# Row numbers of routed tokens: one-hot blocks as weights in all phases instead of a row that is turned

## The chip, the core and the metric

The kernel runs on one core of a Trainium2 chip. The time is that of one launch on the device, in microseconds (us); three runs of the kernel before gave 591.25, 592.46 and 592.63 us, median 592.46. TensorE (PE) multiplies matrices and loads its weights beside that (PEld), VectorE is DVE, ScalarE is ACT, GpSimd is POOL, and SyncE (SP) issues most transfers. Each engine works through its own instructions in order.

## The reference, cut to what matters

Attention with a window and four sink positions gives 1536 tokens of 512 values. They are routed to eight experts, and a second network runs over the result.

```python
cap = N // E                                  # 1536 // 8 = 192
for idx in np.argsort(-(x @ w_gate).flatten()):
    tok, e = idx // E, idx % E
    if assigned[tok] >= 0 or counts[e] >= cap: continue
    assigned[tok] = e; counts[e] += 1
for e in range(E):
    mask = assigned == e
    out[mask] = np.maximum(x[mask] @ w1[e], 0.0) @ w2[e]
# then: h = out @ w_in; g = max(h, 0) + alpha * min(h, 0); result = g @ w_out
```

Every expert receives exactly 192 tokens, so which tokens an expert receives depends on all experts that were full before it.

## The kernel before, in words

**Stages.** Attention comes first. Then eight routing phases (`phase`, s = 0 to 7) each close one expert: compare logits over all tokens still alive, count, pick the expert that is full first, and give its 192 tokens a rank. Phases 0 and 1 look at 12 blocks of 128 tokens, phases 2 and 3 at 9, phases 4 to 7 at 6, because after every second phase (0 and 1, 2 and 3) the living tokens are packed together (`compact`: logits go to memory by indirect transfers on POOL and come back on SP). Expert products (`expert`, L1658 in float32 for experts 0 to 3, L1665 in halves of float16 for experts 4 to 7) and the second network (`chunk`, L1800 and L1843, one chunk for two experts, 384 tokens) run while later phases still route.

**From rank to tokens.** For each block c of a phase DVE makes a one-hot block `o.tile[:, c, a]` of 128 tokens by 192 places in float16 (`hot`, L1325). Both phases of a pair (a = 0, 1) write their half of one buffer `ohs`, of which there is a single one. `gather` (L1470) turns this into token numbers in `sidx`, one number on each partition and three columns for the 384 tokens of a pair: column 0 is filled by the even phase, column 1 by both, 64 numbers each, column 2 by the odd phase. POOL then fetches the tokens' rows from memory with two indirect transfers (L1530), PE turns them (L1543), and the expert's products can begin.

**The two ways to the numbers.** For s >= `BY_ROW` (L1481 to L1500) each block gives one product: weights `tok[:, c:c+1]` (128x1, float16, the token numbers), moving the one-hot block (192 columns), summed over the blocks into one row of 192 on a single partition (L1485). ACT copies the row out of PSUM (L1492), two transposes of 1x128 or 1x64 bring it upright (L1497), and DVE casts it to integers (L1516, L1519, L1521). For s < `BY_ROW` (L1501 to L1514) each block gives two products (only one in phase 0): weights a 128x128 or 128x64 piece of the one-hot pair, moving the token numbers, one column (L1507); the sums stand upright in PSUM and go to the casts at once. In the odd phase the piece for column 1 holds 64 places of either phase, so these products also read the even phase's one-hots. A task covers up to four blocks.

**What sets the order.** All instructions are issued in an order that a planner (`Plan.run`) writes out before the launch. A task has a set of engines, an estimated duration, and a rank: the longest way from it to the end, with `boost` added along the way and `urge` on top of its own rank alone. On each engine the planner takes the task that can start first by its own estimates, and between tasks that can start at the same time the one of the higher rank. `lag` holds a task back by so much behind its inputs. The product tasks of experts and chunks form a chain, so that the earlier ones have the higher rank. Index tasks of the row way have `urge=self.urge(s)` and `lag=self.lag(s)`, which are 300 and 1.0 us for s >= 2, and planned durations of 0.1 us for each block and 0.2 us for the turn. Those of the column way have `urge=self.chain(s)` and a lag of 45 us in phase 0 alone; `chain` is 900 for s = 1 and 0 otherwise; the planned duration is 0.052 us for each block.

**PSUM.** The index sums stand in a bank of the ring `r_r`, which has two. The bank is held from the first product to the last cast. The same ring serves the broadcasts (L1154) and counts (L1221) of the routing and the turned rows (L1543) of phases 1 to 7.

Of the kernel before, what the change touches and what calls it, by code (L numbers as in the profile page):

```python
# [91 lines left out]
class Plan:  # L92
# [11 lines left out]
    def task(self, eng, fn, r=(), w=(), behind=None, after=(), tail=0.0, boost=0.0, nbytes=0, pre=None, bias=None, urge=0.0, port=False, lag=0.0):  # L104

        t = Task()
        t.port = {"DVE": port, "POOL": not tail}
        t.urge, t.lag = urge, lag  # L110
        t.eng, t.fn, t.tail, t.boost, t.n = eng, fn, tail, boost, len(self.tasks)
        deps = set(after)
        t.nbytes, t.pre, t.bias = nbytes, pre, self.BIAS if bias is None else bias
        for x in r:
            deps.update(x.writers)
        for x in w:
            deps.update(x.writers)
            deps.update(x.readers)
        for x in r:
            x.readers.append(t)  # L120
        for x in w:
            x.writers, x.readers = [t], []
        t.bufs = []
        for x in (*r, *w):
            if x.buf is not None:
                if t not in x.buf.users:
                    x.buf.users.append(t)
                if x.buf not in t.bufs:
                    t.bufs.append(x.buf)
        deps.discard(t)  # L130
        t.behind = behind if behind not in deps else None
        if behind is not None:
            deps.add(behind)
        t.deps = list(deps)
        t.succ, t.start, t.end, t.by = [], None, None, None
        for d in t.deps:
            d.succ.append(t)
        self.tasks.append(t)
        return t
# [851 lines left out]
class Routed:  # L991
# [13 lines left out]
    LAND = 4.0  # L1005
    WAIT = 24
    HOT = (40.0,) + (0.0,) * 7
    BY_ROW = 2
    HOLD = {8: 0}
    BY_PE = (0,)  # L1010
    PICK, SET = 300.0, 2000.0
# [260 lines left out]
    def build(self, ctx, w1, w2, weights, out, x16, isv, sv_res):  # L1272
# [197 lines left out]
        def gather(s, st, o, parts):  # L1470
# [9 lines left out]
            rows = ((0, 0, 128), (1, 0, 64)) if not a else ((1, 64, 128), (2, 0, 128))  # L1480
            for x, ro in enumerate(parts) if s >= self.BY_ROW else ():  # L1481

# [6 lines left out]
                named = task({"PE": 0.1 * min(4, nb - 4 * x)}, index, r=[ro, st.t_res], w=got[-1:], urge=self.urge(s), lag=self.lag(s))  # L1489
            if s >= self.BY_ROW:  # L1490
                row, half = idrow[g], idrow[g].part(a)
# [8 lines left out]
                task({"PE": 0.2}, upright, r=[half, idrow[g].part(0)], w=got, urge=self.urge(s), lag=self.lag(s))  # L1500
            for x, ro in enumerate(parts) if s < self.BY_ROW else ():  # L1501

# [498 lines left out]
```

## Time and profile before

| | |
|---|---|
| median of three runs | 592.46 us |
| profiled execution, its own time | 589.01 us |
| span of the profile | 587.1 us |
| PE busy | 549.6 us (94%) |
| DVE busy | 457.3 us (78%) |
| ACT busy | 363.5 us (62%) |
| POOL busy | 156.1 us (27%) |

The profiled execution took 1.9 us more than its span and is 3.45 us below the median. By time the stages are, roughly: attention to 100 us, the first routing phases to 156, experts 0 and 1 to 204, chunk 0 with expert 2 and 3 to 305, chunk 1 to 376, experts 4 and 5 to 413, chunk 2 to 480, experts 6 and 7 to 515, chunk 3 to the end. The index products by row run at six places: 228 (phase 2), 263 (3), 309 (4), 340 (5), 412 (6) and 415 us (7). A busy PE is one whose products are spaced by its own pace, and their ends are modelled; so the cost of a group of products is read from the start of the group to the start of the next instruction.

### The profile page before, as it was taken

The numbers are of one execution on the slowest core, as the hardware profiler recorded it, in microseconds if no ns is written. First come the engines' busy times: TensorE is split into PE (matmuls) and PEld (weight loads), VectorE is DVE, ScalarE is ACT, GpSimd is POOL, SyncE is SP. The second block draws the span as 40 slices with busy tenths as digits, with TensorE's granted clock in tenths as the row PEclk, the third lists the DMA queues.
The fourth block names the chain that finished last, engine by engine and source line by source line (L and its number), as shares of the span: only waits on it lengthen the run. The fifth ranks groups of instructions, "written<-read, shape, count | busy, mean of one in ns | idle before, by whom it ended". The sixth has DMA issues, their size and how long they took to land.

```text
span 587.1 us, 12580 instructions
## 1 busy us (share of the span) xinstructions
PE 549.6 (94%) x4599; PEld 410.0 (70%) x4599; DVE 457.3 (78%) x1299; ACT 363.5 (62%) x757; POOL 156.1 (27%) x244
## 2 busy tenths in 40 slices
PE   6789997599899999999999999999999999999995
PEld 3566776499896688889996555699555569955552
DVE  5989998999777798997799998999995657643321
ACT  6988899586788867576656435565444546442222
POOL 5785945000864313238105010000220000020002
PEclk9989999589999999999999999999999999999998
DMA  8643424166996516335624557565883236110001
GB/s 305 242 128 98 122 74 136 61 216 211 339 354 192 176 37 216 99 108 180 184 85 178 214 188 236 182 213 181 276 280 135 71 111 215 37 55 1 0 1 54
DMA packets 40427, 90.89 MB, mean 155 GB/s; under 512 B 16671, under 2 KB 17294, under 8 KB 40366
## 3 DMA queue, kind: packets, MB, share of 16 engines
q1 hardware_dynamic: 37710, 83.57, 42.5%
q0 software_dynamic: 2656, 6.53, 3.4%
q8 instruction: 36, 0.59, 0.4%
q14 instruction: 25, 0.20, 0.1%
HBM read 81.06 MB, written 6.41 MB: 149 GB/s over the span
## 4 chain that ended last, share of the span: by engine, by line
PE 61%; DVE 13%; issue 12%; ACT 8%; DMA 5%; POOL 2%; POOLq 0%; SPq 0%; DVEq 0%; ACTq 0%
PE o L1843 15%; PE h L1800 15%; PE h L1658 10%; PE h L1665 6%; PE s L523 3%; PE pt L558 3%; DVE spl L1643 2%; DMA r<-w_in 2%; ACT junk L436 1%; ACT spl L1641 1%; DMA xg<-xd,sidx 1%; PE r L1221 1%; DVE cm L1189 1%; DVE ptl L568 1%; PE r L1543 1%
## 5 line engine op out<-in xcount | busy, mean ns | idle before, releaser
L1813 ACT ACTIVATE t<-h,slope 128x384 f32<-128x384 f32 x64 | 37.1, 580 | 75.9 <-PE h L1800 75.9
L1843 PE MATMUL o<-w,gt 128*128 128x512 f16 x324 | 76.6, 379 | 0.0
L1843 PEld LDWEIGHTS <-gt 128*128 128x128 f16 x432 | 41.2, 98 | 43.4 <-issue 0.5
L1665 PEld LDWEIGHTS <-spl 128*128 128x128 f16 x768 | 63.5, 98 | 4.1 <-issue 3.5
L1816 DVE SCALAR_TENSOR_TENSOR v<-h,way,t 128x384 f32<-128x384 f32 x61 | 37.3, 612 | 35.6 <-ACT t L1813 35.4
L1800 PE MATMUL h<-x,w 128*128 128x384 f16 x360 | 63.4, 326 | 0.0
L1800 PEld LDWEIGHTS <-w 128*128 128x128 f16 x360 | 35.1, 98 | 25.4
L1658 PE MATMUL h<-xT,raw 128*128 128x192 f32 x256 | 45.5, 330 | 0.0
L544 ACT ACTIVATE P<-sm,mn 128x260 f32<-128x260 f32 (+1 forms) x96 | 43.1, 490 | 3.1 <-DVE mn L533 2.7
L1658 PE MATMUL h<-h,raw 128*128 128x192 f32 x256 | 44.4, 329 | 0.0
L1643 DVE SCALAR_TENSOR_TENSOR spl<-raw,es,spl 128x1024 f16<-128x1024 f32 x32 | 41.0, 1281 | 4.3 <-ACT spl L1641 4.1
L1889 POOL DMA_INDIRECT out<-ot,sidx x9 | 9.5, 1060 | 129.5 <-ACT ot L1880 97.0
L1820 ACT CAST gt<-v 128x384 f16<-128x384 f32 x48 | 24.5, 510 | 31.0 <-DVE v L1816 29.7
L1530 POOL DMA_INDIRECT xg<-xd,sidx x14 | 17.5, 1250 | 93.2 <-DVE sidx L1521 60.1
L1658 PEld LDWEIGHTS h<-xT,raw 128*128 128x128 f32 x256 | 41.4, 190 | 0.5
L1658 PEld LDWEIGHTS h<-h,raw 128*128 128x128 f32 x256 | 41.3, 190 | 0.1
L533 DVE CUSTOM_DVE_ANT_0 sm<-s,mask 128x260 f32<-128x260 f32 (+1 forms) x96 | 35.4, 397 | 6.1 <-PE s L523 5.7
L1800 PE MATMUL h<-x,vraw 128*128 128x384 f16 x216 | 37.5, 326 | 0.0
L1641 ACT ACTIVATE spl<-raw,es 128x1024 f16<-128x1024 f32 x32 | 36.5, 1143 | 1.4 <-PE h L1665 1.4
L1821 DVE TENSOR_TENSOR gt<-v,gt 128x384 f16<-128x384 f32 x48 | 26.5, 552 | 13.3 <-ACT gt L1820 13.3
L523 PE MATMUL s<-k,q 64*128 64x260 f32 (+1 forms) x192 | 32.6, 433 | 4.3 <-DMA q<-qT 4.3
L1665 PE MATMUL h<-xT,spl 128*128 128x192 f16 x384 | 33.7, 246 | 1.3 <-DVE h L1692 1.1
(314 smaller groups left out, 1315.1 us busy)
## 6 DMA issues: line engine op xcount, KB each, us to landing
raw<-w SPq DMA_DIRECT2D x96, 512.0 KB, 4.3
r<-w_in SPq DMA_DIRECT2D x16, 512.0 KB, 4.1
r<-w_out SPq DMA_DIRECT2D x16, 512.0 KB, 3.8
vraw<-v SPq DMA_DIRECT2D x4, 768.0 KB, 7.7
xd<-x SPq DMA_DIRECT2D x12, 256.0 KB, 2.2
k<-kT SPq DMA_DIRECT2D x11, 260.0 KB, 4.7
q<-qT SPq DMA_DIRECT2D x11, 256.0 KB, 3.0
mrow<-md SPq DMA_DIRECT2D x1, 576.0 KB, 6.5
```

What stands on the lines that cost most here:

```text
L523: nc.tensor.matmul(s.tile[:, :n].rearrange("p (j k) -> p j k", k=KW), lhsT=qs[t].tile[half, p], rhs=kk, start=True, stop=True)
L533: task({"DVE": dve(n)}, lambda: nc.vector.tensor_tensor_reduce(out=sm.tile[:, :n], in0=s.tile[:, :n], in1=mask[:, :n], scale=-0.125, scala ...
L544: task({"ACT": act(n) + 0.137}, lambda h=h, sm=sm, mn=mn: nc.scalar.activation(P[t].tile[:, h, :n], sm.tile[:, :n], AF.Exp, bias=mn.tile, ...
L1641: task({"ACT": act_sb(1024) + 0.09}, lambda: nc.scalar.activation(v(0), src(), AF.Copy, scale=scale()), r=[raw, ws], w=[b.part(0)], lag=se ...
L1643: task({"DVE": dve(1024) + 0.2}, lambda: nc.vector.scalar_tensor_tensor(v(1), src(), scale(), v(0), OP.mult, OP.subtract), r=[raw, ws, b.p ...
L1658: nc.tensor.matmul(ps.tile[:, 0:CAP], lhsT=w[:, k], rhs=x, start=first and k == 0, stop=last and k == 3, skip_group_check=True)
L1665: nc.tensor.matmul(ps.tile[:, 0:CAP], lhsT=w[:, i, k], rhs=xs()[k][:, j], start=first and n == 0, stop=last and n == len(ways) - 1, skip_g ...
L1800: nc.tensor.matmul(ps.tile[:, 0:CH], lhsT=w[:, i, k], rhs=y[j][:, k], start=(n == 0), stop=(n == len(ways) - 1))
L1813: task({"ACT": act(CH)}, lambda: nc.scalar.activation(t.tile, ps.tile[:, 0:CH], AF.Copy, scale=slope), r=[ps, wres], w=[t])
L1816: task({"DVE": dve(CH) + 0.065}, lambda: nc.vector.scalar_tensor_tensor(to(), ps.tile[:, 0:CH], way, t.tile, OP.mult, OP.max), r=[ps, t, w ...
L1821: task({"DVE": dve(CH) + 0.1}, lambda: nc.vector.tensor_tensor(gview(gt)[:, 1], v.tile, gview(gt)[:, 0], OP.subtract), r=[v, gt.part(0)], ...
L1843: nc.tensor.matmul(ops[t].tile, lhsT=gv[:, i, sl], rhs=wv[:, j], start=(f == n == 0), stop=(f == FB - 1 and n == 2))
```

## The change

One constant changes. No phase takes the row way any more.

```diff
-    BY_ROW = 2
+    BY_ROW = 8
```

What phases 2 to 7 issued, and no longer do:

```python
for x, ro in enumerate(parts) if s >= self.BY_ROW else ():
    def index(x=x):
        for c in range(4 * x, min(4 * x + 4, nb)):
            nc.tensor.matmul(ips.tile[0:1, 128:128 + CAP], lhsT=tok[:, c:c + 1], rhs=o.tile[:, c, a], ...)
    named = task({"PE": 0.1 * min(4, nb - 4 * x)}, index, r=[ro, st.t_res], w=got[-1:], urge=self.urge(s), lag=self.lag(s))
if s >= self.BY_ROW:
    task({"ACT": 0.28, "DVE": 0.25}, ...)     # copies the row of 192 out of PSUM
    def upright():
        for j, n in ((0, 128), (1, 64)) if not a else ((1, 128), (2, 128)):
            nc.tensor.transpose(ips.tile[0:n, j:j + 1], row.tile[:, j * 128:j * 128 + n], ident[0:1, 0:1])
```

What they issue now, as phase 1 does already:

```python
for x, ro in enumerate(parts) if s < self.BY_ROW else ():
    def index(x=x):
        for c in range(4 * x, min(4 * x + 4, nb)):
            flat = o.tile[:, c].rearrange("p a t -> p (a t)")
            for j, n in ((0, 128),) if s in self.BY_PE else ((0, 128), (1, 64)) if not a else ((1, 128), (2, 128)):
                nc.tensor.matmul(ips.tile[0:n, j:j + 1], lhsT=flat[:, j * 128:j * 128 + n], rhs=tok[:, c:c + 1], ...)
    named = task({"PE": 0.052 * min(4, nb - 4 * x)}, index, r=[ro, *([parts0[g][x]] if a else []), st.t_res],
                 w=got[-1:], lag=45.0 if s in self.BY_PE else 0.0, urge=self.chain(s))
```

The casts, the fetches and all that follows keep their code. Since the planner writes the order from its estimates, urges and lags, the order of other work from phase 2 on may differ as well.

## Rows read from the trace of the kernel before

**Rows 1.** The page: span, busy time, chain's shares; a group's busy us, mean ns.
```profile
span 587.1 us, 12580 instructions
...
PE 549.6 (94%) x4599; PEld 410.0 (70%) x4599; DVE 457.3 (78%) x1299; ACT 363.5 (62%) x757; POOL 156.1 (27%) x244
...
PE 61%; DVE 13%; issue 12%; ACT 8%; DMA 5%; POOL 2%; POOLq 0%; SPq 0%; DVEq 0%; ACTq 0%
...
L1658 PE MATMUL h<-h,raw 128*128 128x192 f32 x256 | 44.4, 329 | 0.0
```

**Rows 2.** Busy time by stretch: PE, PEld, DVE, ACT, POOL, granted clock, DMA share, GB/s.
```profile
204.00:248.00 44.00, 44.00 (x331) 37.60 (x330) 41.83 (x111) 31.11 (x61) 11.20 (x9) 1.00 0.35 117
248.00:285.00 37.00, 37.00 (x251) 34.31 (x250) 30.38 (x84) 25.80 (x57) 19.23 (x26) 1.00 0.47 143
...
305.00:340.00 35.00, 35.00 (x232) 21.13 (x232) 33.64 (x98) 18.42 (x37) 7.56 (x7) 1.00 0.52 185
340.00:376.00 36.00, 36.00 (x201) 19.24 (x200) 32.30 (x73) 16.69 (x30) 2.53 (x3) 1.00 0.69 229
376.00:386.00 10.00, 8.94 (x131) 8.65 (x129) 9.62 (x21) 5.96 (x13) 0.00 (x0) 1.00 0.45 165
...
420.00:480.00 60.00, 60.00 (x341) 32.97 (x340) 42.68 (x89) 27.13 (x50) 3.91 (x6) 1.00 0.51 177
```

**Rows 3.** The same view, from each row group's start to PE's next instruction.
```profile
228.13:228.97 0.84, 0.84 (x11) 0.67 (x10) 0.28 (x1) 0.67 (x2) 0.00 (x0) 1.00 0.91 351
230.94:231.12 0.18, 0.18 (x4) 0.17 (x3) 0.18 (x1) 0.18 (x1) 0.18 (x1) 1.00 0.12 46
...
414.81:415.39 0.58, 0.58 (x8) 0.41 (x7) 0.47 (x3) 0.00 (x0) 0.00 (x0) 1.00 0.26 106
417.44:417.65 0.21, 0.21 (x4) 0.20 (x3) 0.21 (x1) 0.21 (x1) 0.21 (x1) 1.00 0.17 59
sum 5.16, PE 5.16 PEld 4.04 DVE 3.94 ACT 3.17 POOL 1.43; mean PE 0.43 PEld 0.34 DVE 0.33 ACT 0.26 POOL 0.12
```

**Rows 4.** Timeline of PE, phase 0's column products: start, us, engine, line.
```profile
174.68 2.85 PE L1658 MATMUL h<-h,raw 128*128 128x192 f32 x16
177.37 0.34 PE L1507 MATMUL r<-tok,ohs 128*128 128x1 f16 x8
177.57 1.22 PE L1658 MATMUL h<-h,raw 128*128 128x192 f32 x6
```

**Rows 5.** Timeline of PEld, phase 1's weight loads.
```profile
144.15 0.61 PEld L1507 LDWEIGHTS <-ohs 128*128 128x128 f16 x16
...
145.93 0.41 PEld L1507 LDWEIGHTS <-ohs 128*128 128x128 f16 x8
146.27 0.10 PEld L1337 LDWEIGHTS <-upper 128*128 128x128 bf16 x1
```

**Rows 6.** Timeline of PE, counts inside chunk 1, with 8 columns each.
```profile
311.63 0.31 PE L1221 MATMUL r<-oh,cm 128*128 128x8 bf16 x6
311.80 2.11 PE L1800 MATMUL h<-x,vraw 128*128 128x384 f16 x12
```

**Rows 7.** Timelines of DVE and PE, phase 3 from one-hots to expert.
```profile
260.24 1.70 DVE L1325 TENSOR_SCALAR ohs<-slots,rk 128x192 f16<-128x192 f16 x9
...
263.50 0.90 PE L1485 MATMUL r<-ohs,tok 128*1 128x192 f16 x9
...
266.95 0.16 DVE L1516 CAST sidx<-r 128x2 int32<-128x2 f32 x1 [0.27 <-PE r L1497]
...
279.10 1.04 PE L1543 MATMUL r<-ident,xg 128*128 128x128 f32 x8
...
281.28 1.46 PE L1658 MATMUL h<-xT,raw 128*128 128x192 f32 x8
```

**Rows 8.** Timelines of DVE and PE, phase 4: last one-hots, first index product.
```profile
307.01 0.44 DVE L1325 TENSOR_SCALAR ohs<-slots,rk 128x192 f16<-128x192 f16 x2
...
308.57 0.66 PE L1485 MATMUL r<-ohs,tok 128*1 128x192 f16 x6
```

## The prediction, made before the kernel ran

> **What bounds the kernel now.** I began with the page: PE is busy for 94% of the span, DVE for 78%, and the chain that ended last lies 61% on PE [rows 1]. That is an average over stages, so next I cut the span where the index products lie, and asked of each stretch which engine has no idle time. PE has none in the stretches 204 to 248, 248 to 285, 305 to 340, 340 to 376 and 420 to 480 us, and its granted clock is 1.00, the 2.4 GHz level, in all of them [rows 2]; the clock has no part in this change. The index groups lie in such stretches, but for the last two, at 412 to 418 us, where chunk 2 begins. So an index product is not hidden there: PE time that is saved lets every later product start earlier. The reader should also see the second engine: DVE has only 0.4 us of idle time in the 10 us from 376, where PE for once idles (8.94 of 10) [rows 2]. That is where a gain could be lost.
>
> **What goes.** I read the cost of the row way from the start of each group to the start of PE's next instruction. Twelve places: six groups of row products (9 or 6 blocks) and six pairs of transposes. Phase 2 pays 0.84 us for nine products and 0.18 us for the turn, phase 7 0.58 us for six and 0.21 us; the twelve add up to 5.16 us of PE time [rows 3]. A product of this kind thus costs 0.093 us. A little more hangs on it: PE sits a moment ahead of the transposes. I put that at 0 to 0.5 us in all and count 0. Six copies of a row leave ACT; ACT is idle for 12.9 of 44 us in the first stretch and more after that [rows 2], so they count nothing in themselves.
>
> **What comes.** Two products for each block: 2 x 9 x 2 + 4 x 6 x 2 = 84, each with weights of 128x128 (or 128x64) and one moving column. The trace has such products in phases 0 and 1. Eight of them stand between float32 expert products: 16 of these start within 2.85 us less the 0.329 us that one lasts [rows 1, 4], so 0.168 us apart, the last at 177.20; the next expert product began at 177.57. Of these 0.37 us 0.168 would have passed anyway, so eight column products moved it by 0.20 us, 0.025 us each [rows 4]. The nearest row inside a chunk, where four of the six phases stand, is a count: six products of 128x128 weights and 8 columns, 0.17 us from first start to the next product, 0.028 us each [rows 6]. From the other side, by weight loads: 16 last 0.61 us in all and one of them 0.10, so they start 0.034 us apart; eight run from 145.93 to 146.27, 0.042 each [rows 5]. I take 0.027, between the two rows that show displaced products: 84 x 0.027 = 2.3 us. The bounds are 84 x 0.025 = 2.1 and 84 x 0.042 = 3.5 us.
>
> **A rule that speaks against it.** The rows show that a 128-column load of float16 begins 0.034 to 0.042 us after the one before it [rows 5]. The Trainium skill ("TensorE: Matmul & The Clock Gate", section "LDWEIGHTS (loading the stationary operand)") puts a load at its columns divided by 1.2, in ns, which for 128 columns is 107 ns, and says that only the columns matter. By that, 84 loads would take 9.0 us, an estimate from that page, against 42 loads of one column now, and the change would lose; here the trace does not agree.
>
> **The sum.** 5.16 - 2.3 = 2.9 us less PE time, between 1.6 (dear products) and 3.6 us (0.025 us each and the 0.5 us ahead of the transposes). Phases 2 to 5 give 3.62 - 60 x 0.027 = 2.0 us of it, phases 6 and 7 (0.75 and 0.79 us, [rows 3]) 1.54 - 24 x 0.027 = 0.9 us.
>
> **The shorter way to the tokens.** Copy and turn also leave the way from one-hots to fetch. In phase 3 the products begin at 263.50, the cast stands at 266.95, the fetched rows are turned at 279.10 and expert 3 begins at 281.28 [rows 7]. The cast could come some 2.5 us earlier. That is worth nothing by itself, since PE is busy with expert 2 until then; it only adds room, and so I cost it at nothing. If the cover were gone, a late fetch would cost PE its delay one for one. The two fetches may now be put ahead of the compaction's transfers on POOL instead of between them. Those, and the load of the packed logits behind them on SP, could be late by two fetches at most, while expert 4, the first to need them, starts some 90 us later. The `r_r` bank is held shorter, which helps phase 3's broadcasts. Phases 4 to 7 have tens of us between index and expert. No wait is added for POOL or SP. The index tasks of an odd phase also wait for the even phase's one-hots, which are long done.
>
> **Urge and lag.** What else changes is the place of these tasks on PE. They lose an urge of 300 and a lag of 1.0 us. With the urge gone, the planner weighs them against chunk products by the length of their way to the end. In phases 2 and 3 the expert is under 20 us off and the fetch, turn and boosts lie in between, so I expect them to go first still; in phases 4 to 7 they may be put back by some products, which costs nothing there. With the lag gone they may be put too early. That is the second rival.
>
> **Rivals.** (A) The gain is lost at 376 us. Experts 4 and 5 need split weights and low halves, which DVE makes, and DVE is 96% busy from 376 to 386 [rows 2]. If PE gets there 2.0 us earlier and DVE doesn't, PE waits 2.0 us more, and only phases 6 and 7 pay: 592.46 - 0.9 = 591.6. For it speaks DVE's 93% in the two stretches before; against it that 5.1 of those 71 us are idle on DVE, and that part of its work at 376 belongs to a phase that isn't due. (B) PE waits for one-hots, and the kernel is slower. Place: the index tasks of phases 2 to 7. PE is in order, so an index product that arrives before its one-hots holds back all expert and chunk products, and with them ACT and DVE, which take their results. One-hots end at 261.94 and the products start at 263.50 in phase 3, 1.56 us later; in phase 4 it is 307.45 and 308.57, 1.12 us [rows 7, 8]. 1.0 us of this is the lag that goes. If the plan runs ahead of DVE by another half group of products (a group is 2.11 us, [rows 6]), PE waits about 1.05 us a phase, 6.3 us in all: 592.46 - 2.9 + 6.3 = 595.9. It decides from 2.9 us on, 0.5 us a phase. Against it: phase 1 has the column way without a lag, and its eight last loads pass at 0.042 us each with no hole [rows 5]. (C) Weight loads bind: each of the 84 products costs what one load lasts, 0.10 us as in [rows 5], 8.4 us. Then it is 592.46 + 8.4 - 5.16 = 595.7. This is what the page's rule amounts to. Against it stand the spacings above.
>
> **How the numbers follow.** The sum is made on an execution of 589.01 us (span 587.1 and 1.9 around it), which would come to 586.1; set against the median of 592.46, the forecast is 589.6 us. Its own bounds are 588.9 and 590.9. Chances: forecast 0.43, A 0.26, B 0.28, C 0.03. A measurement of this kernel can tell about 0.3%, 1.8 us, from no change. The forecast is faster than that but for its dear end, A is within it, B and C are slower: 0.43, 0.26, 0.31. The range of 8 in 10 must reach over A to B's centre at 595.9, and below the forecast to 586.0, since a new order can also close waits that these rows don't show: 586.0 to 596.0.
>
> **What would show it.** Right: no row products, copies or transposes in phases 2 to 7; 84 more column products at 0.025 to 0.035 us each; PE busy time 2 to 3 us lower; casts of phase 3 within 1.5 us of its index products; expert 4's first product about 2 us earlier and the end about 3. A shows as more idle time on PE ahead of L1665 after 376 us with DVE as releaser. B shows as idle time ahead of L1507 released by the one-hots of L1325, or as a hole right there. C shows as 0.1 us from start to start. The prediction is wrong if the planner's new order moves other work, such as DVE's splits or an expert's start, so that PE idles at a place that has nothing to do with index products.

## The result, and the profile after

The kernel got slower: 594.26 us (median of 21 runs, 590.98 to 599.83) against 591.89 us of the kernel before (21 runs, 586.88 to 594.44), a ratio of 1.0062 with a 95% interval of 1.0039 to 1.0086. The medians lie 2.4 us apart; by the ratio, which is taken from all the runs, the kernel takes about 3.7 us more, where 2.9 us less was forecast. The profiled execution of the changed kernel took 593.88 us. Its page begins so (compare [rows 1]); the second line has busy us, share of the span and instructions of each engine, the third the shares of the chain that ended last:

```profile
span 591.9 us, 12628 instructions
...
PE 555.4 (94%) x4629; PEld 413.6 (70%) x4629; DVE 459.2 (78%) x1302; ACT 359.6 (61%) x746; POOL 152.1 (26%) x243
...
PE 61%; DVE 14%; issue 11%; DMA 7%; ACT 4%; POOL 2%; SPq 0%; POOLq 0%; DVEq 0%; ACTq 0%
```

PE has 5.8 us more busy time than in [rows 1], not 2 to 3 us less. That number says little, though: 5.3 us of it lie in the first 217 or 218 us, where both kernels run the same 2014 products in the same order (190.06 us busy before, 195.39 after). The busy time by stretch of the changed kernel, with the columns of [rows 2]:

```profile
204.00:248.00 44.00, 43.98 (x335) 37.71 (x334) 40.04 (x108) 30.45 (x61) 11.70 (x9) 1.00 0.33 107
...
285.00:305.00 20.00, 18.02 (x142) 17.31 (x142) 16.73 (x50) 11.65 (x26) 0.00 (x0) 1.00 0.40 135
...
376.00:386.00 10.00, 10.00 (x113) 8.31 (x111) 9.16 (x25) 6.19 (x12) 0.00 (x0) 1.00 0.60 185
420.00:480.00 60.00, 59.24 (x340) 32.02 (x339) 45.96 (x94) 26.05 (x47) 7.35 (x10) 1.00 0.56 192
```

Where [rows 2] had PE idle, at 376, it is now busy; between 285 and 305 it now idles for 2 us and after 420 for 0.8 us. Before, it was full after 420 and idled for 0.4 us in the other stretch:

```profile
285.00:305.00 20.00, 19.60 (x151) 18.76 (x151) 17.14 (x51) 11.97 (x25) 0.00 (x0) 1.00 0.32 109
```

And this is what took the place of [rows 3]: the same view of the six index groups, phases 2 to 7, each from its first product to PE's next other instruction (the fifth line has eight of phase 6's twelve products, the last one has the other four and all twelve of phase 7):

```profile
232.25:234.32 2.07, 2.07 (x20) 1.81 (x19) 0.56 (x1) 2.07 (x5) 1.62 (x2) 1.00 0.83 265
264.42:264.88 0.46, 0.46 (x19) 0.46 (x19) 0.42 (x4) 0.26 (x1) 0.00 (x0) 1.00 1.03 419
314.53:315.90 1.37, 1.37 (x13) 1.20 (x12) 1.37 (x5) 0.75 (x2) 0.83 (x1) 1.00 0.75 308
349.03:349.34 0.31, 0.31 (x14) 0.31 (x13) 0.31 (x2) 0.19 (x1) 0.00 (x0) 1.00 0.09 27
414.97:415.88 0.91, 0.91 (x10) 0.73 (x9) 0.82 (x5) 0.32 (x1) 0.00 (x0) 1.00 0.71 234
420.14:421.07 0.93, 0.90 (x17) 0.70 (x16) 0.53 (x4) 0.67 (x2) 0.64 (x1) 1.00 0.79 313
sum 6.05, PE 6.02 PEld 5.21 DVE 4.01 ACT 4.25 POOL 3.09; mean PE 1.00 PEld 0.87 DVE 0.67 ACT 0.71 POOL 0.51
```

The first two lines hold 18 products of the same kind each. Phase 2 pays 2.07 us for them and phase 3 0.46: 0.115 against 0.026 us. The phases differ in one thing, which the timeline merges and the view of the source line shows (shape, count): an odd phase loads weights of 128 columns only, an even one turns from 128 to 64 columns and back with each block.

```profile
L1507 PEld LDWEIGHTS <-ohs x120: 95/96/106, 146.5 to 420.9; 128*128 128x128 f16 x99, 128*64 128x64 f16 x21
```

To place the rest, I cut both traces at three points of the program that a new order leaves in place: the 61st product of L1800 (217.08 us before, 218.20 after), expert 4's first product of L1665 (375.7, 379.2) and expert 6's (479.1, 483.9). The view of busy time over the first stretch, before and then after (length, PE busy):

```profile
217.08:375.70 158.62, 158.22 (x1038) 119.89 (x1037) 142.16 (x382) 94.85 (x191) 39.18 (x45) 1.00 0.51 172
```

```profile
218.20:379.20 161.00, 158.65 (x1060) 120.69 (x1059) 142.76 (x377) 92.34 (x187) 35.87 (x45) 1.00 0.51 166
```

So up to expert 4 the changed kernel lost 2.4 us: 0.4 of PE work and 1.95 of idle time on PE. From there to expert 6 it lost 1.3 us (103.4 before, 104.7 after), nearly all idle time (1.71 before, 2.98 after). Behind that both take 108.0 us. The other 1.1 us lie ahead of the first of the three points, and they say nothing of the change: in two more profiles of the changed kernel this point lies at 218.91 and 224.01 us, in one more of the kernel before at 225.12.

The idle time of the first stretch has a name. In the list of who waits for whom (us in all, times, longest), from 200 us on, the changed kernel has first:

```profile
PE h L1734 <- DVE tm L1732: 2.9, 2, 2.0
PE h L1665 <- DVE h L1692: 1.9, 2, 1.3
PE h L1665 <- DVE xm L1739: 0.9, 1, 0.9
```

and the kernel before, among others:

```profile
PE h L1665 <- DVE h L1692: 2.0, 5, 0.6
...
PE h L1734 <- DVE tm L1732: 0.9, 1, 0.9
```

So the waits for L1692 are no larger than before in all; new are 2.0 us ahead of L1734, which lie in the first stretch, and 0.9 us ahead of L1665 (expert 5), which lie in the second. The timelines of PE and of DVE in the changed kernel (start, us; in brackets idle time and releaser) show how the larger one comes about:

```profile
284.95 1.47 PE L1658 MATMUL h<-xT,raw 128*128 128x192 f32 x8
288.39 0.21 PE L1734 MATMUL h<-ident,tm 4*128 4x4 f32 x1 [1.98 <-DVE tm L1732]
```

```profile
284.44 0.35 DVE L1723 TENSOR_REDUCE xm<-h 128x1 f32<-128x192 f32 x1
287.50 0.20 DVE L1125 TENSOR_REDUCE m<-L 128x6 f32<-128x48 f32 x1 [2.72 <-DMA L<-cd]
...
288.07 0.27 DVE L1732 TENSOR_REDUCE tm<-h 4x1 f32<-4x128 f32 x1
```

DVE stands in its order at the packed logits of chunk 1 (L1125), for which it waits 2.7 us. Expert 2's small reduction (L1732) is queued behind it, and PE waits for that reduction. The kernel before had the same two instructions the other way round, and DVE's wait for the logits cost PE little (0.4 us, at L1154):

```profile
283.07 0.27 DVE L1732 TENSOR_REDUCE tm<-h 4x1 f32<-4x128 f32 x1
...
287.14 0.20 DVE L1125 TENSOR_REDUCE m<-L 128x6 f32<-128x48 f32 x1 [2.01 <-DMA L<-cd]
```

So there are two suspects: the price of the new products, and the new order.

### The profile page after: what moved, and what is told of

Its sections match the earlier page's. It is cut to its first block, busy times and chain, and to the rows that moved or that the text cites. A ratio compares the mean times of both kernels' runs of the same rounds, so it can differ in the third digit from the quotient of the medians.

```text
span 591.9 us, 12628 instructions
## 1 busy us (share of the span) xinstructions
PE 555.4 (94%) x4629; PEld 413.6 (70%) x4629; DVE 459.2 (78%) x1302; ACT 359.6 (61%) x746; POOL 152.1 (26%) x243
## 4 chain that ended last, share of the span: by engine, by line
PE 61%; DVE 14%; issue 11%; DMA 7%; ACT 4%; POOL 2%; SPq 0%; POOLq 0%; DVEq 0%; ACTq 0%
PE o L1843 15%; PE h L1800 14%; PE h L1658 9%; PE h L1665 8%; PE s L523 5%; PE pt L558 4%; DMA r<-w_in 2%; DMA cd<-L,ids 2%; DVE spl L1643 1%; DMA xg<-xd,sidx 1%; PE r L1221 1%; DVE cm L1189 1%; DVE cm L1174 1%; DVE ptl L568 1%; PE pv L609 1%
## 5 line engine op out<-in xcount | busy, mean ns | idle before, releaser
L1843 PE MATMUL o<-w,gt 128*128 128x512 f16 x324 | 77.2, 379 | 0.6 <-DVE gt L1821 0.4
L1843 PEld LDWEIGHTS <-gt 128*128 128x128 f16 x432 | 41.1, 98 | 43.8 <-DVE gt L1821 0.9
L1665 PEld LDWEIGHTS <-spl 128*128 128x128 f16 x768 | 63.4, 98 | 4.1 <-issue 3.7
L1800 PE MATMUL h<-x,w 128*128 128x384 f16 x360 | 63.4, 326 | 0.0
L1800 PEld LDWEIGHTS <-w 128*128 128x128 f16 x360 | 35.1, 98 | 25.9
L1658 PE MATMUL h<-xT,raw 128*128 128x192 f32 x256 | 45.7, 330 | 0.0
L1658 PE MATMUL h<-h,raw 128*128 128x192 f32 x256 | 44.6, 329 | 0.0
L1658 PEld LDWEIGHTS h<-xT,raw 128*128 128x128 f32 x256 | 41.3, 190 | 0.4 <-DVE xT L1466 0.3
L1658 PEld LDWEIGHTS h<-h,raw 128*128 128x128 f32 x256 | 41.3, 190 | 0.2
L523 PE MATMUL s<-k,q 64*128 64x260 f32 (+1 forms) x192 | 36.3, 476 | 4.1 <-DMA q<-qT 4.1
L1800 PE MATMUL h<-x,vraw 128*128 128x384 f16 x216 | 37.8, 326 | 0.2
L1665 PE MATMUL h<-xT,spl 128*128 128x192 f16 x384 | 33.5, 246 | 2.4 <-DVE h L1692 1.3
L558 PE MATMUL pt<-ident,P 128*128 128x128 f32 x176 | 31.0, 299 | 4.3 <-DVE ptl L568 2.6
```

Of the source, the lines that this page charges most:

```text
L523: nc.tensor.matmul(s.tile[:, :n].rearrange("p (j k) -> p j k", k=KW), lhsT=qs[t].tile[half, p], rhs=kk, start=True, stop=True)
L558: nc.tensor.transpose(o[:, a, g], P[t].tile[:, 2 * p + a, g * KW:g * KW + 128], ident)
L1658: nc.tensor.matmul(ps.tile[:, 0:CAP], lhsT=w[:, k], rhs=x, start=first and k == 0, stop=last and k == 3, skip_group_check=True)
L1665: nc.tensor.matmul(ps.tile[:, 0:CAP], lhsT=w[:, i, k], rhs=xs()[k][:, j], start=first and n == 0, stop=last and n == len(ways) - 1, skip_g ...
L1800: nc.tensor.matmul(ps.tile[:, 0:CH], lhsT=w[:, i, k], rhs=y[j][:, k], start=(n == 0), stop=(n == len(ways) - 1))
L1843: nc.tensor.matmul(ops[t].tile, lhsT=gv[:, i, sl], rhs=wv[:, j], start=(f == n == 0), stop=(f == FB - 1 and n == 2))
```

## The experiments

My theory was that the change of width between neighbouring loads costs 0.09 us each time and that this, with what follows from it, is the loss. The rivals were the planner's order (urge and lag lost, DVE at L1125 ahead of L1732) and the clock. In two of the four groups of runs (all experiments up to the later look) even the kernel before takes 601 to 602 us; in its profile there PE idles for 2.3 us ahead of L1658 near 287, and each variant of these groups has a wait of 2.1 to 3.1 us on PE that ends between 285 and 297. Each ratio is therefore to the kernel before in the same group of runs.

**The kernel before, once more, and all loads 128 wide.** The second pass of an even phase takes the full 128 places. The upper 64 belong to the odd half; they are set to zero ahead of the one-hots, on POOL, and the 64 added sums are not read.

```
-((0, 128), (1, 64)) if not a else ((1, 128), (2, 128))
+((0, 128), (1, 128)) if not a else ((1, 128), (2, 128))
+nc.gpsimd.memset(o.tile[:, 0:nb, 1, 0:64], 0.0)   # s in (2, 4, 6)
```

> The kernel before once more, profiled beside the experiments. Both theories: no wait over 1 us ahead of L1730 or L1734 near 284 us, row products at 0.58 to 0.84 us a group as in its first trace, no fall of the granted clock after 135 us.

> The changed kernel in its own order, but the 64-place pieces of phases 2, 4 and 6 are loaded as 128 columns (the odd phase's half of the one-hots is cleared on POOL first; the rows it adds are never read). Width theory: a load of 64 columns between loads of 128 makes every product of the even phases cost 0.115 us instead of 0.025; with 128 the 42 products of phases 2, 4 and 6 take 1.1 us instead of 4.8, PE gets 3.7 us back, and the time falls to that of the kernel before (ratio 0.999 to 1.002). Order theory: what the change lost lies in waits of PE for DVE that the new order brought (2.1 us ahead of L1734 at 286 us, 1.5 us ahead of L1665 at 402 us, 1.5 us in chunk 2 at 420 to 428 us); these stay or grow as PE comes earlier, and the ratio stays at 1.004 or more.

The wide kernel took 600.08 against 601.06 us, 0.9985 [0.9946, 1.0024]; the single run of the kernel before took 601.78 us, and, other than expected, its granted clock fell twice after 135 us, at 160.9 and at 287.2. Between the traces, the index products up to expert 4 take 3.62 us by rows and 1.55 us wide, 2.1 less, and the stretch up to expert 4 is 163.3 and 161.0 us, 2.3 less. In the products, the gain that the prediction saw for phases 2 to 5 (2.0 us) is there once the widths are equal. In the stretch it isn't always whole: two later profiles of the wide kernel have 157.8 and 157.1 us, 0.8 and 1.5 less than the first trace of the kernel before (158.6). The interval reaches 2.3 us to either side, so it holds 1 for a gain of this size.

**The same loads, sorted by width.** The two loops change places, so four loads of 128 stand together and then four of 64.

```
-for c in range(4 * x, min(4 * x + 4, nb)):
-    for j, n in ...:
+for j, n in ...:
+    for c in range(4 * x, min(4 * x + 4, nb)):
```

> The changed kernel in its own order, but within each task of up to four blocks all first pieces come before all second pieces, so that in even phases four loads of 128 columns are followed by four of 64. If the change of width from load to load is what is slow: all products start 0.025 to 0.03 us apart but for one or two per task, and phase 2's 18 take 0.7 us instead of 2.07. If a load of 64 columns is slow by itself: the 128s start 0.025 us apart, the 64s still over 0.1, and phase 2 takes about 1.3 us. If width has nothing to do with it: still 2.07. Time: 1 to 3.5 us below the changed kernel by the width theory.

Phase 2's 18 products, in the same view as above:

```profile
237.06:238.09 1.03, 1.03 (x19) 0.94 (x18) 0.56 (x1) 1.03 (x3) 1.03 (x2) 1.00 0.78 107
```

They take 1.03 us instead of 2.07, with the same 18 loads of the same sizes; 0.7 was expected. The starts of the single products tell more, and why it isn't 0.7: loads of 128 follow each other by 25 ns (the first two of a run by 39 to 42); the first of 64 comes 93 ns after the last of 128; the next ones by 53, 32 and 31 ns; the first of 128 after them by 102 or 103 ns. In the changed kernel's phase 2 the steps are 107 to 111 and 120 to 123 ns in turn, without exception. So neither a load of 64 nor one of 128 is dear by itself; the change from one to the other is, and the next one or two loads still pay a little. The time was 599.77 us, 0.9962 [0.9922, 1.0003].

**The place of the tasks, from both sides.** First the row way with the column way's urge and no lag, then the column way with the row way's urge and lag.

```
-... index, r=[ro, st.t_res], w=got[-1:], urge=self.urge(s), lag=self.lag(s))
+... index, r=[ro, st.t_res], w=got[-1:], urge=self.chain(s))
```

(and the same for `upright`);

```
-w=got[-1:], lag=45.0 if s in self.BY_PE else 0.0, urge=self.chain(s))
+w=got[-1:], lag=45.0 if s in self.BY_PE else self.lag(s), urge=self.chain(s) if s < 2 else self.urge(s))
```

> The kernel before with its row products, copy and transposes, but their tasks have the urge (0) and the lag (0) of the column way in phases 2 to 7; only the planned order differs. Order theory: slower by 2 to 4 us, ratio 1.003 to 1.007, with waits such as the one ahead of L1734 near 286 us. Width theory: within 1.5 us of the kernel before, ratio 0.998 to 1.0025.

> The changed kernel, column products with the 64-column loads kept, but with the urge (300) and lag (1.0 us) that the row way had. Order theory: the waits go and the time returns to that of the kernel before (ratio 0.998 to 1.002). Width theory: PE still pays 5.9 us for the index products against 5.16 us by row, so it is 0.7 us slower than before by that, and the 3 us of waits stay or are replaced by others; ratio 1.001 to 1.006, index products of phases 2, 4 and 6 0.115 us apart.

The row way without its urge took 611.4 us, 1.0153 [1.0094, 1.0211], though its products are the old ones. The three longest of its waits on PE that have no counterpart in the profile of the kernel before that took 601.78 us:

```profile
PE h L1665 <- DVE spl L1643: 2.1, 3, 0.8
PE h L1658 <- ACT xf L1709: 2.1, 1, 2.1
...
PE h L1408 <- DVE h L1692: 2.1, 1, 2.1
```

None of them has to do with the index. So a new order alone can cost 1.5%, far more than the 0.3 to 0.7% that was expected. The changed kernel with the old urge and lag took 602.73 us, 1.004 [0.9998, 1.0082]: its products cost 4.20 us up to expert 4, as dear as in the changed kernel (4.21). So urge and lag are not what made the products dear. The time settles nothing: its interval reaches into the ranges of both theories.

**Chunk 1's first look at the logits, put later.** The planner is told that the reduction of L1125 and the copy of L1375 can begin 2.4 us later, so that L1732 goes ahead of them.

```
-seq.append(task({"DVE": dve(n * E)}, head, r=lb, w=[m.part(a)], urge=soon))
+seq.append(task({"DVE": dve(n * E)}, head, r=lb, w=[m.part(a)], urge=soon, lag=2.4 if s == 4 else 0.0))
```

(and the same lag for the copy).

It is made on the changed kernel, on the wide one, and on the kernel before as the control.

> The changed kernel, with two DVE tasks that read the packed logits of phase 4 (L1125 and L1375) planned 2.4 us later, so that they stand behind the maxima of expert 2 (L1723, L1732) in DVE's order and not ahead of them. Wait theory: the changed kernel loses 2.1 to 3.2 us because PE waits ahead of L1730 or L1734 for DVE, and DVE for the packed logits; this wait goes, the 64-column loads stay (2.07 us in phase 2), and the ratio to the kernel before is 0.999 to 1.004, some 0.004 below the changed kernel. If another wait takes its place, the ratio stays at 1.005 or more.

> Both at once: 128-column loads in the even phases and the two DVE tasks 2.4 us later. Index products cost 2.2 us in all instead of 5.9, no wait ahead of L1730 or L1734. If the forecast of 2.9 us less than the kernel before was right but for the load width and this wait, the ratio is 0.993 to 0.997. If the gain is always lost at a later wait, it is 0.998 or more.

> The kernel before, row way, with the same two DVE tasks 2.4 us later. Its trace shows 0.56 us of PE waiting there, so wait theory: ratio 0.997 to 1.001. If planning these tasks later is good by itself, whatever the index products, the ratio is 0.996 or less.

Times and ratios: 601.86 us, 0.9997 [0.9956, 1.0038]; 600.36 us, 0.9966 [0.992, 1.0012]; 608.57 us, 1.0107 [1.0054, 1.016]. The control is the lesson: the same edit makes the kernel before 1.1% slower. Its list of waits has 2.1 us of PE for `xT` (L1547), against 0.4 us in the kernel before in that group of runs. Going later is not good in itself; each new plan is a new draw of waits. On the changed kernel the edit settles nothing: its profile still has 1.8 us of waiting ahead of L1730.

**Dear and cheap in one order.** Then the changed kernel, the wide one, and the wide one with the later look and with the old urge besides, all in one group of runs.

> The changed kernel itself, beside its own variants on one chip. Width theory: 1.2 us (0.002) or more above the wide variant timed beside it, and 3 us (0.005) or more if nothing is eaten by later waits; ratio to the kernel before 1.002 to 1.008 as in its first measurement. If the width made no difference, it equals the wide variant.

> The changed kernel with 128-column loads in the even phases, timed again beside the changed kernel. Width theory: index products of phases 2 to 7 cost about 2.2 us instead of 5.9; the time lies 1.2 to 3.7 us below the changed kernel. Order theory: same time as the changed kernel within 1 us.

> 128-column loads and the two DVE tasks on phase 4's packed logits planned 2.4 us later, timed again. Width theory plus order: its new order has no waits of chunk 2 at 420 to 430 us, so the whole 2.9 us of the forecast should show: ratio to the kernel before 0.993 to 0.997. If gains in index products are eaten elsewhere: 0.998 or more.

> As the one before it, and the index tasks have the urge of 300 and the lag of 1.0 us of the row way. If urge and lag matter by themselves, this is 1 us or more faster than the variant without; if order only shuffles waits, it is within 3 us either way, with waits at other places. Index products cost 2.2 us in all in either case.

| variant | us | ratio to before, 95% |
|---|---|---|
| changed kernel again | 597.34 | 1.0108 [1.0069, 1.0147] |
| wide | 590.69 | 0.9981 [0.9943, 1.002] |
| wide, later look | 590.99 | 0.9971 [0.9927, 1.0015] |
| wide, later look, old urge and lag | 590.32 | 0.9981 [0.994, 1.0022] |

The first two have the same tasks with the same urge, and both keep the wait ahead of L1734 in their profiles (1.91 and 1.46 us). Their traces even have PE's other 4509 products in one and the same order, and so have the sorted kernel and the two doubled ones below: between these kernels the planner's order is no rival. The width of the second load makes 6.65 us between the first two by the medians, 1.27% by the ratios. The products themselves explain 3.7: 42 of them at 0.115 instead of 0.026 us. How much of that reaches the end can be read from the distance between fixed points of this order, in three profiles of the changed kernel (the first one, this one and one more below) and two of the wide one (us):

| from, to | changed | wide |
|---|---|---|
| first product of phase 2, of phase 3 | 32.17, 33.72, 32.18 | 30.53, 30.52 |
| phase 3, phase 4 | 50.11, 51.72, 48.84 | 49.60, 48.92 |
| phase 4, phase 5 | 34.50, 34.50, 34.50 | 33.42, 33.42 |
| phase 5, phase 6 | 65.94, 65.94, 65.93 | 65.94, 65.94 |

The products make 1.6 us in phase 2 and 1.1 in phase 4, and, read in the same way from the products around it, 0.6 in phase 6: 3.3 of 3.7 us reach the end, in every profile. What varies beside that is the second row, where the wait ahead of L1734 lies, and the first row in the second profile. The rest of the way behind phase 2 agrees within 0.03 us. The traces show what happened in that second profile. The changed kernel's index group of phase 2, and the stretch behind it (the granted clock is third from the right):

```profile
232.96:235.03 2.07, 2.07 (x19) 1.81 (x18) 0.56 (x1) 2.07 (x5) 1.62 (x2) 1.00 0.85 237
236.40:239.80 3.40, 3.40 (x11) 3.01 (x10) 2.48 (x7) 1.14 (x2) 2.97 (x2) 0.51 0.29 77
```

and the wide kernel's:

```profile
234.00:234.47 0.47, 0.47 (x20) 0.47 (x19) 0.47 (x1) 0.47 (x2) 0.47 (x1) 1.00 0.63 113
237.40:240.80 3.40, 3.40 (x34) 2.75 (x33) 3.40 (x10) 0.69 (x2) 1.58 (x2) 1.00 0.39 116
```

After 2.07 us of products with one moving column the clock granted to PE fell to the 1.2 GHz level for 3.4 us; after 0.47 us of them it did not. In the first profile of the changed kernel it did not fall there, and that is the difference between 33.72 and 32.17 us in the table: the fall cost 1.55 us. The changed kernel here has a second stretch of 0.51, from 291.10 to 294.50, behind the wait ahead of L1734; by the second row of the table (51.72 against 50.11, with waits of 1.91 and 1.98) it cost 1.6 us. The wide kernel has none in spite of its wait.

In the wide, later kernel PE doesn't wait at L1734 (its timeline of PE):

```profile
287.27 1.47 PE L1658 MATMUL h<-xT,raw 128*128 128x192 f32 x8
288.66 0.21 PE L1734 MATMUL h<-ident,tm 4*128 4x4 f32 x1
```

Its stretches are 156.2 us to expert 4 and 102.7 to expert 6, 3.1 us less than before: in the trace the forecast gain. The times can't show it: the ratio came out at the upper end of the 0.993 to 0.997 that was expected, and its interval holds 1. It beats the changed kernel; that it beats the kernel before is not settled. The old urge and lag on top make no difference that the times show (590.32 against 590.99 us).

**The disputed price, doubled.** In both widths each product of an even phase is made twice, the second time into a column that nobody reads. The order of tasks stays.

```
 begun.append(c)
+[nc.tensor.matmul(ips.tile[0:n, 64 + j:65 + j], lhsT=flat[:, j * 128:j * 128 + n], rhs=tok[:, c:c + 1], start=False, ...)
+ for j, n in ((0, 128), (1, 64)) if s in (2, 4, 6)]     # wide: (1, 128)
```

> The changed kernel with the index products of phases 2, 4 and 6 made twice, the second time into PSUM columns that nobody reads: 42 more products of changing width. Width theory: 0.115 us each, 4.8 us more PE time; if it reaches the end one for one the ratio to the kernel before rises by 0.008 over the changed kernel's, to 1.014 to 1.020, and more if the granted clock falls behind the slow products. If the width is harmless: 0.025 us each, 1.05 us, ratio 1.007 to 1.012.

> The wide variant with the index products of phases 2, 4 and 6 made twice in the same way, all with 128-column loads. Width theory: 42 more products at 0.025 us, 1.05 us, ratio 0.998 to 1.003. If the number of products is what costs, not the change of width, it loses as much as the variant of changing width, 4 us or more.

> One more profile of the changed kernel. If slow products of changing width draw the clock down, it falls to half for a stretch within 4 us of the end of phase 2's index products, as in one of its two profiles so far; if that was chance, it doesn't.

> One more profile of the wide variant. The clock stays at its upper level behind phase 2's index products, by either account; a fall there would end the idea that changing width draws it down.

Doubled as it was made, 603.08 us, 1.0227 [1.0184, 1.0269]; doubled wide, 593.2 us, 1.0056 [1.0022, 1.0091]. Phase 2's 36 products in the one and in the other:

```profile
231.37:235.51 4.14, 4.14 (x37) 3.62 (x36) 0.56 (x1) 2.87 (x6) 1.62 (x2) 1.00 0.43 133
```

```profile
228.25:229.17 0.92, 0.92 (x38) 0.92 (x37) 0.56 (x1) 0.92 (x2) 0.92 (x2) 1.00 0.92 107
```

0.115 against 0.0256 us a product; 84 of them make 7.5 us of the 9.9 us between the kernels. The narrow one has half clock twice, each time behind an even phase:

```profile
235.50:238.90 3.40, 3.40 (x12) 3.39 (x12) 3.28 (x11) 0.00 (x0) 2.54 (x2) 0.50 0.29 73
320.80:324.20 3.40, 3.40 (x18) 1.70 (x17) 2.00 (x8) 1.12 (x2) 2.02 (x3) 0.51 0.25 67
```

By the distances from phase 2 to 3 (35.76 against 31.00 us) and from 4 to 5 (37.49 against 33.72), less what the products explain, each fall cost 1.5 to 1.6 us: 10.7 in all, a little over what was timed. The wide doubled kernel cost more than the 1.05 us of its products; its profile has 2.31 us of waiting ahead of L1734, and I can't say more of it. The single runs of the changed kernel and the wide one gave 598.16 and 592.01 us, the wide one again ahead; the clock fell behind phase 2 in neither profile.

In all, the clock fell behind an even phase in 3 of 6 profiles with alternating widths (the changed kernel's second, the doubled one, the one with the later look) and in 0 of 12 with rows, wide or sorted products. That makes it likely that slow index products bring it about; six profiles don't prove it, and what else must come together is open. Falls of the same or twice the length stand elsewhere too, with rows and with any width of load: between 157 and 175 and between 204 and 219 us ahead of phase 2, and, behind idle time on PE, between 286 and 302, at 413 (the later look) and at 416 us (the row way without its urge, both ahead of phase 6); they are no part of this count.

## Why the prediction was wrong

**The step that failed is "What comes".** The mechanism, products for products on a PE that is full, was right; the term was mis-sized. 84 products were put at 2.3 us, with bounds of 2.1 and 3.5. They cost 6.05 us, so the step gave no 2.9 us back but cost 0.9. The half of them in odd phases came as forecast: 18 in 0.46 us (0.026 each) and 12 in 0.31. The 42 in even phases cost 4.8 us instead of 1.1. [Rows 4] and [rows 5] show loads of 128x128 in a row and nothing else, and [rows 6] too. The text names the 128x64 loads in its own first sentence on the matter, and then prices them by rows that have none. The trace showed no float16 loads of 128 and 64 columns in turn, and there the bound should have reached, from the nearest row that was not of the same kind, up to what one load lasts, 0.10 us in [rows 5]: that was rival C, with a chance of 0.03.

**The rule that speaks against it.** The Trainium skill's 107 ns for a load of 128 columns ("TensorE: Matmul & The Clock Gate", section "LDWEIGHTS (loading the stationary operand)") is close to the steps in the even phases, 107 to 123 ns, but not for its reason: loads of the same width, 128 columns, follow each other by 25 ns, and narrower ones made it dear. The prediction's estimate by that formula was also too high: 21 of the 84 loads have 64 columns, 53 ns each by the formula, which makes 7.9 us instead of 9.0. The same page, section "Weight-path perf modes — Fast Weight Load (FWL) and DoubleRow", says that a faster load of weights asks for the full 128 columns and a type other than float32. The trace agrees as far as it can: with that condition met throughout, a product costs 0.026 us, with it met by every second load 0.115. That 64s in a row also come 31 ns apart is not in it. I had read the section that spoke against the change and not the one that named its condition.

**The sum.** 2.9 us were to go and 3.7 came, a miss of 6.6 by the ratio (5.3 by the medians). Mis-sized products are 3.8 of it (0.9 instead of -2.9, by the views), and that the width is the reason is shown, by kernels that issue the same products in the same order. For the remaining 1.5 to 2.8 the traces offer the order and the clock, and no run divides it between them: the trace pair has 1.95 and 1.27 us more idle time on PE in the two stretches, the first at L1734, the second ahead of L1665 in expert 5 (2.2 us, 0.8 more than before) and at L1843 (0.6 us), and no fall of the clock; the second profile of the same kernel has two falls of 1.6 us each. So the sentence that the clock has no part in this change, read from a trace without such products, does not hold in every execution.

**Rival A** (the gain is lost at 376 us) did not come where it was put: PE is full from 376 to 386, and the changed kernel had no gain to lose. The wide kernel has one up to expert 4, and there something like A does happen, a little later: from expert 4 to expert 6 it takes 104.1 us against 103.4 before, with 3.7 us of idle time on PE against 1.7, of which 2.2 against 1.4 lie ahead of L1665 behind DVE. In the wide kernel with the later look this stretch takes 102.7, and the gain stays. **Rival B** (PE waits for one-hots) did not come: in its list of waits no product of L1507 waits for L1325, and phase 2's products even go 5 us after their one-hots. Its number, 595.9, was near the result by luck, for another reason. **Rival C** gave 595.7 and had the right place and very nearly the right price, for half of the products.

**The shorter way to the tokens** came as told and was worth nothing, as told: phase 3's products begin at 264.42 and its cast stands at 265.70, 1.3 us later instead of 3.45 in [rows 7].

**Urge and lag.** The prediction ended on the right warning, that a new order might let PE idle at a place that has nothing to do with index products, and gave it no price. L1734 is that place. The runs put the size of such a thing at up to 1.5% of the kernel, by an edit that changes no work (the row way without its urge) or next to none (the later look).

What stays open: how the loss beyond the products divides between waits and clock in a typical execution, and whether the wide kernel, with or without its variants, is really faster than the kernel before (its five ratios lie between 0.9966 and 0.9985, and each interval holds 1).

## What to carry to other kernels

A price taken from a row holds for the sequence that the row shows: ask not only what an instruction costs but what stands next to it, and whether the new code changes sizes from one to the next. Weights of one width in a row, padded or sorted, cost a fraction of weights that alternate. And where a planner sets the order, run the edit's order without its work, or its work in the old order, before the difference is put down to the work. If two kernels have the same order, compare their traces between fixed points: here most of these distances repeat within 0.03 us, where the times of one kernel scatter by some us.

## What the runs showed of the hardware

- The price of a product with one moving column lies in the change of width of its weights: 25 ns from 128 to 128 columns, 93 ns from 128 to 64, 31 to 53 ns from 64 to 64, 102 to 103 ns from 64 to 128, and 107 to 123 ns at every step when they alternate (float16, granted clock 1.00; phase 2 of the sorted and of the changed kernel; the first two loads of a run of 128 are 39 to 42 ns apart). Only these two widths were tried.
- The duration that the trace gives to one load does not show it: 95 to 106 ns for all 120, dear and cheap (the changed kernel's L1507). Only the distance from start to start does.
- Two microseconds or more of such alternating products were followed within 1.5 us by 3.4 us at the 1.2 GHz level in 3 of 6 profiles; behind the same work, wide or sorted, there was none in 8. A fall behind phase 2 cost 1.55 us (33.72 against 32.17).
